# MoE1's second matmul by Strassen's seven products for eight of its twelve token chunks, and the other four chunks spread through MoE2

## The chip, the cores and the metric

One program on one core of a Trainium2 chip. The time is device microseconds of one execution; three executions of the kernel before gave 1471.46 to 1471.69 us, median 1471.59. A separate execution was profiled; its rows are shown below.

## The reference

Three stages in a row, all on float32 inputs and outputs (the MoE weights arrive as float64 words):

```python
scores = (1 / S) * z @ z.T                 # per batch; S = 3008, d_qk = 64
x = u * (maximum(scores, 0) ** 2 @ v)      # 2 x 3008 tokens, d_model = 256
h = maximum(x @ moe_w_in, 0)               # MoE1, d_ff = 2048
x = h * h @ moe_w_out
h = x @ moe2_w_in                          # MoE2, d_ff = 2048
y = (h - tanh(h)) @ moe2_w_out
```

## The kernel before

**Number format.** TensorE multiplies in a reduced float32 format (`F32R`). To keep accuracy every operand is split into a high part and a low part, and each product is three matmuls: high x high, low x high, high x low. The split costs a copy (ScalarE or VectorE) and a subtraction (VectorE) for each operand tile.

**Tiles.** The 6016 tokens are cut into 12 attention chunks (`chunks`, up to 512 tokens) and, for both MoE stages, into 12 even `groups`: four of 512 tokens and eight of 496. `d_ff` is cut into `NF` = 16 blocks of 128. One MoE step is a pair (chunk, block) and has two runs of six matmuls on TensorE:

- `front(i)` (L531): x times one block of w_in into one PSUM bank `s`, 2 halves of d_model x 3 terms;
- `back(i)` (L608): the block's activation `h` times w_out into the two accumulators `o` of the chunk, 2 halves of d_model x 3 terms.

Between them ScalarE and VectorE make `h` out of `s`. In MoE1: `bend` (L543, Relu out of PSUM, ScalarE), `power` (L546, Square, ScalarE), `high` (L589 on ScalarE or L591 on VectorE, the high part), `rest` (L594, the low part, VectorE). In MoE2 there are two activations and a square on ScalarE (L552, L543, L555), a difference, a mask, a product and a selection on VectorE (L560, L571, L579, L582), then `high` and `rest`; once MoE1 has no steps left the mask moves to ScalarE (L567).

**PSUM.** A core has eight banks of 512 float32 columns. In the MoE stages four serve `front` in rotation (pool `pf`), four serve as accumulators `o` (pool `po`).

**Order of the steps.** First all attention steps, then MoE1 and MoE2 steps: 41 MoE1 steps ahead, after which MoE2 and MoE1 steps alternate; 21 MoE2 steps remain alone at the end. MoE1's result of a chunk goes from PSUM straight into the split operand of MoE2 (`between`, L624 and L626).

**Who decides the order on each engine.** `plan` writes TensorE's order by hand (`order_p`): a front stands three steps ahead of its back (`LOOK`), four in the end. For the other engines it makes a `Job` for each operation with a due time, the pools that it takes and the work that it waits for, and `drive` lays them in order, engine by engine, by its own table of durations. The built program then holds a fixed order on each engine; nothing is decided at run time. An engine whose next instruction is not ready waits, and all behind it wait too.

**Weights.** Each weight block is loaded as float64 words, converted and split by a chain of three ScalarE and six VectorE instructions (`split_w`). The 16 blocks of MoE1 and ten of them by way of DRAM (`wd`) are prepared during attention and fetched back; MoE2's are prepared in the MoE stages.

Of the kernel before, what the change touches and what calls it, by code (L numbers as in the profile page):

```python
# [31 lines left out]
EARLY = 1  # L32
WARM = 13
# [9 lines left out]
def kernel(  # L43
# [40 lines left out]
    def width(kind, c):  # L84
        return chunks[c][2] if kind == "att" else groups[c][1]
# [63 lines left out]
    wd = dp.tile([KEEP0 + KEEP1, P, 2, 512], F32, name="wd")  # L149
# [8 lines left out]
    def load_v(b, j):  # L158

        if b == 0 and 3 <= j < 6:  # L160
            pool, tag = (wp, "w") if j == 5 else (rawp, "raw")
            raw = pool.tile([P, 2, D], F32, tag=tag, name="vraw")
        else:
            raw = ap_.tile([P, 2, D], F32, tag="a", name="vraw")
        if j < NV - 1:
# [27 lines left out]
    def split_z(b, t, raw):  # L193
# [4 lines left out]
        if b == t == 0:  # L198
# [30 lines left out]
    def split_w(m, f, keep, raw):  # L229
        if keep is None:  # L230
            w = wt["w", m, f] = wp.tile([P, 2, 512], F32R, tag="w", name="ww")
        else:
            if len(stage) < 2:
                stage.append(wp.tile([P, 2, 512], F32R, tag="w", name="wk"))
            w = stage[keep % 2]
        if w1_in.dtype == F32:
# [32 lines left out]
    def load_x(c):  # L269
        t0, n = groups[c]  # L270
        x = xp.tile([P, KD, NMAX], F32, tag="x", name="xr")
        SP.dma_start(out=x[:, :, :n], in_=xd[:, :, t0 : t0 + n])
        return x

    def split_x(c, x, u):
        t0, n = groups[c]
        if c >= EARLY:
            y = slice(max(done_u - t0, 0), n)
            yield "V", lambda: V.tensor_mul(x[:, :, y], x[:, :, y], u[:, :, y])
        xh, xl = new_xs(0, c)  # L280
# [6 lines left out]
    order = [(m, f) for m in range(2) for f in range(NF)]  # L287
    keeps = {STAY + k: k for k in range(KEEP0 + KEEP1)}
    split = STAY + KEEP0 + KEEP1

# [11 lines left out]
    end = at["m1", NCH - 1, NF - 1] + 1  # L302
    limit = (TC * math.tanh(TB * TH)) ** 2
# [94 lines left out]
    def opening(both):  # L398
# [4 lines left out]
        first("z", 1)  # L403
        A.activation(a[:, 0], a[:, 0], AF.Square)
        first("z", 1)
# [110 lines left out]

    def front(i):
        kind, c, k = steps[i]
        n = groups[c][1]
        if not single:  # L520
            s_pool.close()
            single["s"] = ctx.enter_context(
                tc.tile_pool(name="pf", bufs=4, space=bass.MemoryType.PSUM)
            )
        s = got[i] = single["s"].tile([P, NMAX], F32, tag="s", name="s")
# [90 lines left out]
    def between(c, d, e):  # L616

        n = groups[c][1]
        if d == 0 and e == "A":
            new_xs(1, c)  # L620
        xh, xl = xs[1, c]
        o = acc["m1", c][d][:, :n]
        if e == "A":
            A.activation(xh[:, d, :n], o, AF.Copy)  # L624
        else:
            V.tensor_sub(xl[:, d, :n], o, xh[:, d, :n])  # L626

    def out(c, d, e):

        n = groups[c][1]  # L630
        if d == 0:
            xt["y", c] = xp.tile([P, KD, NMAX], F32, tag="x", name="y")
        y, o = xt["y", c][:, d, :n], acc["m2", c][d][:, :n]
# [5 lines left out]
    def send(c):  # L639
# [4 lines left out]
            in_=xt["y", c][:, :, :n],  # L644
        )

    def send_last():
# [3 lines left out]
        y, o = xt["y", c], acc["m2", c]  # L651
        SP.dma_start(out=yT[:P, t0 : t0 + n], in_=y[:, 0, :n])
        A.activation(y[:, 1, :n], o[1][:, :n], AF.Copy)
        A.dma_start(out=yT[P:, t0 : t0 + n], in_=y[:, 1, :n])

    class Job:
# [26 lines left out]
        "f": [0.0] * 4,  # L683
# [38 lines left out]
    def best(e):  # L722
# [4 lines left out]
        if e == "P":  # L727
            return (max(free[e], ready(jobs[0])), jobs[0])
# [71 lines left out]
    def plan(first_steps):  # L800

        order_p, ahead = [], 2
        for n in range(at["m1", 0, 0]):
            until = min(n + (APART if n > 6 else 2), at["m1", 0, 0] - 1)
# [11 lines left out]
        ahead = at["m1", 0, 0]  # L816
        for n in range(ahead, len(steps)):
# [7 lines left out]
        for kind, i in order_p:  # L825
            when[kind, i] = t
            if kind[0] == "o":
# [89 lines left out]
        for k, (m, f) in enumerate(order):  # L917
# [8 lines left out]
            else:  # L926
                t0, t1 = when["f", at["m1", 0, 0]], when["f", at["m2", 0, 0]]
                need = t0 + 6.0 + (k - split + 1) * (t1 - t0 + 10.0) / (2 * NF - split)
                need, asks = min(need, when["f", at["m2", 0, f]] - 4.0), at["att", NCH - 1, 0] + 10
# [7 lines left out]
            fresh = kept is None or kept < 2  # L937
            owed[0] += fresh
# [6 lines left out]
            def begin(k, made=made, fresh=fresh):  # L945
                if k == 0:
                    owed[0] -= fresh
                made(k)
            jobs = chain(W, need, after, ["t", "t"] + ["w"] * fresh, give, begin)
            wjob[m, f] = jobs[-1]  # L950
            if kept is not None:
# [3 lines left out]
                last = (NCH - 1) * NV  # L955

                def bring(e, pools, m=m, f=f, kept=kept):
# [5 lines left out]
                    when["f", at["m1", 0, f]] - 12.0,  # L963
                    [(last + min(kept + 2, NV - 1), 0.0), (stages[-1], 0.0)],
                    ["w"],
                    S=2.6,
                )
        xjob, xhold = {}, {(m, c): hold("z") for m in range(2) for c in range(NCH)}
        for c in range(NCH):
            need = when["f", at["m1", c, 0]]  # L970
            x, u = [None], [None]
            xs_, us_ = hold("x"), hold(None)
            asks = at["m1", c - 1, 2] if c else (NCH - 1) * NV + 4

            def ask(e, pools, c=c, x=x):
                x[0] = load_x(c)

            def ask2(e, pools, c=c, u=u):
# [323 lines left out]
```

## Time and profile before

| | before |
|---|---|
| median of three executions | 1471.59 us |
| the profiled execution | 1471.73 us |
| its span in the trace | 1469.9 us |
| TensorE matmul busy | 1464.5 us |
| VectorE busy | 1232.2 us |
| ScalarE busy | 1070.1 us |
| granted TensorE clock | 1.00 of 2.4 GHz |

The profiled execution's time is 1.83 us above its span, which is the time that lies around the traced program. Busy time counts a stretch once, however many instructions of the engine overlap in it.

### The profile page before, as it was taken

What the parts mean: (1) busy time and instruction counts of PE and PEld (TensorE: products, weight loads), DVE (VectorE), ACT (ScalarE), POOL (GpSimd) and SP (SyncE); (2) the same over time, 40 slices, a digit from 0 to 9 for tenths busy, and PEclk for the clock granted to TensorE, in tenths of its full rate; (3) what the DMA queues carried; (4) which work ended last, traced back from release to release, by engine and by line L of the source; (5) the groups of instructions that cost most, each with busy time, mean ns of one, the idle gap of its engine ahead of it and who ended that gap; (6) DMA issues with size and microseconds to landing.
All of it is one profiled execution on the core that took longest, in us unless ns stands there. A gap on an engine that the chain in (4) does not pass through costs nothing.

```text
span 1469.9 us, 21919 instructions
## 1 busy us (share of the span) xinstructions
PE 1464.5 (100%) x8499; PEld 1230.9 (84%) x8499; DVE 1232.2 (84%) x1846; ACT 1070.1 (73%) x1698; POOL 0.3 (0%) x6
## 2 busy tenths in 40 slices
PE   9999999999999999999999999999999999999998
PEld 7888888888898888888888888888888888888887
DVE  7888999788986888877888888888888888888788
ACT  8987669987648987666666667676666766666688
POOL 0000000000000000000000000000000000000000
PEclk9999999999999999999999999999999999999999
DMA  8756648766663321010100100010101010000000
GB/s 256 249 193 219 207 154 262 266 216 212 218 244 95 119 91 38 1 42 1 43 1 1 42 1 15 1 42 1 42 1 43 1 42 1 14 1 15 1 14 15
DMA packets 74200, 125.67 MB, mean 85 GB/s; under 512 B 4720, under 2 KB 56688, under 8 KB 70256
## 3 DMA queue, kind: packets, MB, share of 16 engines
q1 hardware_dynamic: 73792, 123.76, 25.2%
q8 instruction: 66, 1.08, 0.3%
q10 hardware_dynamic: 304, 0.52, 0.1%
q14 instruction: 38, 0.31, 0.1%
HBM read 75.24 MB, written 49.02 MB: 85 GB/s over the span
## 4 chain that ended last, share of the span: by engine, by line
PE 96%; ACT 3%; DVE 1%; issue 0%
PE s L531 33%; PE o L608 33%; PE o L480 25%; PE s L431 4%; ACT h L589 1%; ACT least L567 1%; ACT a L543 1%; ACT f L552 0%; PE o L452 0%; ACT f L555 0%; PE s L1225 0%; DVE a L582 0%; PE s L416 0%; DVE a L560 0%; DVE g L579 0%
## 5 line engine op out<-in xcount | busy, mean ns | idle before, releaser
L608 PE MATMUL o<-h,ww 128*128 128x496 f32 (+1 forms) x2304 | 574.0, 385 | 0.4 <-DVE h L594 0.4
L531 PE MATMUL s<-xs,ww 128*128 128x496 f32 (+1 forms) x2304 | 573.9, 385 | 0.0
L608 PEld LDWEIGHTS o<-h,ww 128*128 128x128 f32 x2304 | 432.4, 188 | 80.3 <-DVE h L594 0.8
L531 PEld LDWEIGHTS s<-xs,ww 128*128 128x128 f32 x2304 | 432.3, 188 | 79.9 <-issue 0.3
L543 ACT ACTIVATE a<-s 128x496 f32<-128x496 f32 (+1 forms) x384 | 226.2, 589 | 155.7 <-PE s L531 154.1
L480 PE MATMUL o<-h,vw 64*128 64x512 f32 (+1 forms) x2240 | 339.3, 382 | 0.0
L594 DVE TENSOR_TENSOR h<-a,h 128x496 fp32r<-128x496 f32 (+1 forms) x384 | 248.4, 677 | 18.9 <-ACT h L589 14.7
L480 PEld LDWEIGHTS o<-h,vw 64*128 64x128 f32 x2240 | 209.9, 184 | 39.6
L560 DVE TENSOR_TENSOR a<-s,a 128x496 f32<-128x496 f32 (+1 forms) x192 | 130.3, 679 | 107.6 <-ACT a L543 106.7
L480 PE MATMUL o<-l,vw 64*128 64x512 f32 (+1 forms) x1120 | 214.1, 382 | 0.0
L552 ACT ACTIVATE f<-s 128x496 f32<-128x496 f32 (+1 forms) x192 | 114.1, 595 | 111.0 <-PE s L531 110.2
L589 ACT ACTIVATE h<-a 128x496 fp32r<-128x496 f32 (+1 forms) x219 | 136.9, 627 | 21.5 <-DVE a L582 8.2
L582 DVE COPY_PREDICATED a<-small,f 128x496 f32<-128x496 uint8 (+1 forms) x171 | 125.5, 734 | 5.1
L546 ACT ACTIVATE a<-a 128x496 f32<-128x496 f32 (+1 forms) x192 | 119.6, 623 | 5.6
L480 PEld LDWEIGHTS o<-l,vw 64*128 64x128 f32 x1120 | 105.0, 184 | 20.4 <-DVE l L371 0.8
L337 DVE STREAM_TRANSPOSE at<-m 128x1024 f32<-128x1024 f32 x60 | 121.8, 2030 | 0.0
L555 ACT ACTIVATE f<-f 128x496 f32<-128x496 f32 (+1 forms) x192 | 121.2, 631 | 0.0
L579 DVE TENSOR_TENSOR f<-s,f 128x496 f32<-128x496 f32 (+1 forms) x171 | 116.3, 680 | 5.1
L371 DVE TENSOR_TENSOR l<-a,h 128x1024 fp32r<-128x1024 f32 (+1 forms) x83 | 100.6, 1215 | 19.9 <-ACT h L362 19.5
L362 ACT ACTIVATE h<-at 128x1024 fp32r<-128x1024 f32 (+1 forms) x60 | 61.4, 1023 | 47.7 <-PE o L480 42.2
L591 DVE CAST h<-a 128x496 fp32r<-128x496 f32 (+1 forms) x165 | 69.1, 421 | 26.9 <-PE o L608 14.0
L393 ACT ACTIVATE a<-a 128x1024 f32<-128x1024 f32 (+1 forms) x83 | 87.3, 1054 | 1.3
(57 smaller groups left out, 824.3 us busy)
## 6 DMA issues: line engine op xcount, KB each, us to landing
ad<-a SPq DMA_DIRECT2D x60, 512.0 KB, 3.8
m<-ad SPq DMA_DIRECT2D x30, 1024.0 KB, 7.0
wraw<-in_moe_w_in_dram SPq DMA_DIRECT2D x32, 256.0 KB, 4.2
wraw<-in_moe_w_out_dram SPq DMA_DIRECT2D x32, 256.0 KB, 4.2
vraw<-in_v_dram SPq DMA_DIRECT2D x22, 256.0 KB, 4.8
wd<-wk SPq DMA_DIRECT2D x10, 512.0 KB, 4.3
ww<-wd SPq DMA_DIRECT2D x10, 512.0 KB, 9.5
xd<-e SPq DMA_DIRECT2D x9, 512.0 KB, 3.4
```

The costliest lines, as they stand in the source:

```text
L337: V.transpose(a.rearrange("p g (k j m) -> p m k g j", k=4, m=4), m.rearrange("p (m k) (t g i) -> t p m k g i", m=4, t=2, g=2)[p % 2],)
L480: T.matmul(o[r * KD + d][:, :n], lhsT=w[halves[r], hl, g * D + d * P : g * D + (d + 1) * P], rhs=mv[halves[r], g, :n], start=x == 0 and (r ...
L531: T.matmul(s[:, :n], lhsT=w[:, hl, kd * P : (kd + 1) * P], rhs=mv[:, kd, :n], start=j == 0, stop=j == len(seq) - 1,)
L543: A.activation(a, got[i][:, :n], func)
L546: A.activation(sq[i], sq[i], AF.Square)
L555: A.activation(fs[i], fs[i], AF.Square, scale=TC)
L560: V.tensor_sub(sq[i], got[i][:, :n], sq[i])
L579: V.tensor_mul(gs[i], got[i][:, :n], f)
L582: V.copy_predicated(sq[i], least[i], gs[i])
L589: A.activation(pair[i][:, 0], sq[i], AF.Copy)
L594: V.tensor_sub(pair[i][:, 1], sq[i], pair[i][:, 0])
L608: T.matmul(o[d][:, :n], lhsT=w[:, side, (KD + d) * P : (KD + d + 1) * P], rhs=mv, start=k == 0 and j % 3 == 0, stop=k == NF - 1 and j % 3 ...
```

## The change

Chunks 0 to 7 of MoE1 are taken in four pairs. For a pair, two blocks of d_ff and the two halves of d_model, the second matmul is a product of 2 x 2 blocks (two chunks by two blocks of d_ff, times two blocks of d_ff by two halves of d_model). Strassen's form (with Winograd's sums) makes it with seven block products in place of eight. A window ("w", r, j) is one such step: pair r of 4, block pair j of 8; there are 32.

A window has four fronts (L557, as before six matmuls each) and seven products (L632, three matmuls each). `rise` (L572 on ScalarE, L574 on VectorE) and `rise2` (L577) are the Relu and the Square; `less` (L581) makes the four differences of activations; `upper` (L588, or L590 on VectorE) and `lower` (L593) split each of the seven operands; `sums_w` makes the four sums of w_out blocks once for each j; `gather` (L647 to L667) combines the seven accumulators at the end of a pair, and `lay` stores the result to DRAM (`x2d`).

The seven accumulators take all four banks of `po` and three more (pool `pg`), so that one bank (`pf`) is left for the fronts of a window. After the phase, `many(i)` lets fronts rotate over `pg` and `pf` again.

The 64 MoE1 steps of chunks 8 to 11 are no longer alternating with MoE2 one to one: 16 stand ahead, the other 48 are spread over 167 of the 192 MoE2 steps (`LEAD`), and 25 MoE2 steps remain alone at the end. All of MoE1's results go to MoE2 through DRAM (`x2d`, `put_x`, `load_x`), and `between` is gone. Twelve of MoE2's weight blocks are converted in the new phase, four after it.

In the opening, scores of chunk 0 are recorded ahead of some loads, the second z tile's high part is a VectorE cast in place of a ScalarE copy, and a one-column memset holds back one load of v. In the ending, the last half of the output is copied by VectorE in two pieces that leave by two queues.

```diff
+PAIRS = 4
+DIRECT = 6
+LEAD = 16
+PRODUCTS = 1, 5, 7, 3, 6, 2, 4
+LATE = 3, 8, 14
...
     steps = [("att", c, x) for c in range(NCH) for x in range(NV)]
-    m1 = [("m1", c, k) for c in range(NCH) for k in range(NF)]
+    FFN = len(steps)
+    steps += [("w", r, j) for r in range(PAIRS) for j in range(NF // 2)]
+    m1 = [("m1", c, k) for c in range(2 * PAIRS, NCH) for k in range(NF)]
     m2 = [("m2", c, k) for c in range(NCH) for k in range(NF)]
-    lead = 2 * NF + LAG + 4
-    steps += m1[:lead]
-    given = lead
+    given = 0
     for i in range(len(m2)):
-        steps.append(m2[i])
-        ahead = lead - (NF + 4) * min(max(i - 2 * NF, 0), 8 * NF) // (8 * NF)
-        while given < min(len(m1), i + 1 + ahead):
+        while given < min(len(m1), LEAD + i * (len(m1) - LEAD) // (len(m2) - NF - LAG - 4)):
             steps.append(m1[given])
             given += 1
+        steps.append(m2[i])
...
+    def bank(many):
+        if not single:
+            s_pool.close()
+            for name, bufs in ((False, 1), (True, 3)):
+                single[name] = ctx.enter_context(
+                    tc.tile_pool(name="pg" if name else "pf", bufs=bufs, space=bass.MemoryType.PSUM)
+                )
+        return single[many].tile([P, NMAX], F32, tag="s", name="s")
...
+    def less(i, q, x, y):
+        V.tensor_sub(tiles[i, q], tiles[i, x], tiles[i, y])
...
+    def sums_w(j):
+        val = tp.tile([P, 512], F32, tag="t", name="val")
+        s = tp.tile([P, 512], F32, tag="t", name="sw")
...
+        yield "V", lambda: V.tensor_add(s1, a21, a22)
+        yield "V", lambda: V.tensor_sub(s3, a11, a21)
+        yield "V", lambda: V.tensor_sub(s2, s1, a11)
+        yield "V", lambda: V.tensor_sub(s4, a12, s2)
+        w = st[j] = wp.tile([P, 2, 512], F32R, tag="w", name="ws")
+        yield "A", lambda: A.activation(w[:, 0, :], s, AF.Copy)
+        yield "V", lambda: V.tensor_sub(w[:, 1, :], s, w[:, 0, :])
...
+    def product(i, p, part):
+        _, r, j = steps[i]
+        n = groups[2 * r][1]
+        if j == 0 and part == 0:
+            sb[r, p] = (
+                po.tile([P, NMAX], F32, tag="o", name="o") if p in (1, 5, 7, 3) else bank(True)
+            )
+        x = sb[r, p]
+        h = pair[i, p]
...
+        terms = ((0, h[:, 0]), (1, h[:, 0]), (0, h[:, 1]))
+        for y in (0, 1) if part == 0 else (2,):
+            hl, mv = terms[y]
+            T.matmul(
+                x[:, :n],
+                lhsT=w[:, hl, d * P : (d + 1) * P],
+                rhs=mv,
+                start=j == 0 and y == 0,
+                stop=j == NF // 2 - 1 and y == 2,
+            )
...
     def send_last():
...
-        A.activation(y[:, 1, :n], o[1][:, :n], AF.Copy)
-        A.dma_start(out=yT[P:, t0 : t0 + n], in_=y[:, 1, :n])
+        for way, cols in ((A, slice(0, n // 2)), (SP, slice(n // 2, n))):
+            V.tensor_copy(y[:, 1, cols], o[1][:, cols])
+            way.dma_start(out=yT[P:, t0 : t0 + n][:, cols], in_=y[:, 1, cols])
...
+        order_p += [(("f", q), FFN) for q in (0, 3, 1, 2)]
+        ahead = two
+        for n in range(FFN, two):
+            spots = {3: 0, 8: 1, 14: 2, 18: 3}
+            count = 0
+            for p in PRODUCTS:
+                for part in range(2):
+                    order_p.append((("p", p, part), n))
+                    count += 2 - part
+                    if count not in spots:
+                        continue
+                    if n + 1 < two:
+                        order_p.append((("f", spots[count]), n + 1))
```

What this makes of TensorE's order: before, in the 41 MoE1 steps ahead, a front of six and a back of six follow one another (the back alternates between the chunk's two accumulators, each row one matmul):

```order
L531 MATMUL s_6250<-xs_6075,ww_1479 128x512 x6
L608 MATMUL o_6209<-h_6219,ww_914 128x512
L608 MATMUL o_6210<-h_6219,ww_914 128x512
L608 MATMUL o_6209<-h_6219,ww_914 128x512
L608 MATMUL o_6210<-h_6219,ww_914 128x512
L608 MATMUL o_6209<-h_6219,ww_914 128x512
L608 MATMUL o_6210<-h_6219,ww_914 128x512
```

Now TensorE in one window of the third pair (`o_7425`, `o_7448`, `o_7455`, `o_7471`, `s_7479`, `s_7501`, `s_7518` are the accumulators of products 1, 5, 7, 3, 6, 2, 4; the other `s` are fronts, all in the one bank of `pf`):

```order
L632 MATMUL o_7425<-h_7565,ww_1244 128x496 x3
L557 MATMUL s_7631<-xs_7004,ww_5508 128x496 x6
L632 MATMUL o_7448<-h_7597,ws_5836 128x496 x3
L632 MATMUL o_7455<-h_7617,ws_5836 128x496 x2
L557 MATMUL s_7657<-xs_7170,ww_5508 128x496 x6
L632 MATMUL o_7455<-h_7617,ws_5836 128x496
L632 MATMUL o_7471<-h_7609,ws_5836 128x496 x3
L632 MATMUL s_7479<-h_7638,ws_5836 128x496 x2
L557 MATMUL s_7685<-xs_7170,ww_5536 128x496 x6
L632 MATMUL s_7479<-h_7638,ws_5836 128x496
L632 MATMUL s_7501<-h_7644,ww_1484 128x496 x3
L557 MATMUL s_7704<-xs_7004,ww_5536 128x496 x6
```

Between two fronts stand five, six and four matmuls of products (and, from the last front to the first of the next window, 3 + 3 = 6). The fronts belong to the next window, the products to this one. This pattern stands in 29 of the 32 windows; in three a product or a part of one has moved past a front.

VectorE at about the same place, where the operands of one window are made (`b` are activations, `wraw`, `mant`, `exp` and `wk` a weight block that is converted):

```order
L593 TENSOR_TENSOR h_7575<-b_7521,h_7575 128x496
L581 TENSOR_TENSOR b_7548<-b_7570,b_7548 128x496
L261 SCALAR_TENSOR_TENSOR exp_7394<-wraw_7052,exp_7394 128x512
L590 CAST h_7597<-b_7548 128x496
L264 TENSOR_TENSOR mant_7395<-mant_7395,exp_7394 128x512
L581 TENSOR_TENSOR b_7570<-b_7592,b_7570 128x496
L593 TENSOR_TENSOR h_7597<-b_7548,h_7597 128x496
L590 CAST h_7617<-b_7570 128x496
L581 TENSOR_TENSOR b_7548<-b_7592,b_7548 128x496
L593 TENSOR_TENSOR h_7617<-b_7570,h_7617 128x496
L593 TENSOR_TENSOR h_7609<-b_7592,h_7609 128x496
L593 TENSOR_TENSOR h_7638<-b_7548,h_7638 128x496
```

Before, VectorE had for the same MoE1 blocks only the low parts, one for each front, and sometimes a high part:

```order
L591 CAST h_6248<-a_6229 128x512
L594 TENSOR_TENSOR h_6248<-a_6229,h_6248 128x512
L594 TENSOR_TENSOR h_6260<-a_6243,h_6260 128x512
L594 TENSOR_TENSOR h_6287<-a_6269,h_6287 128x512
```

## Rows read from the trace of the kernel before

**Rows 1.** The page, part 1: span, and busy time, share, instructions of each engine.

```profile
span 1469.9 us, 21919 instructions
PE 1464.5 (100%) x8499; PEld 1230.9 (84%) x8499; DVE 1232.2 (84%) x1846; ACT 1070.1 (73%) x1698; POOL 0.3 (0%) x6
```

**Rows 2.** TensorE's waits after its first instruction: total us, times, longest.

```profile
PE o L608 <- DVE h L594: 0.4, 1, 0.4
PE s L431 <- ACT z L201: 0.4, 1, 0.4
```

**Rows 3.** Stages in time: busy us by engine, then PEclk, DMA share, GB/s.

```profile
441.00:1415.00 974.00, 974.00 (x4385) 821.96 (x4382) 799.50 (x1373) 681.12 (x1211) 0.00 (x0) 1.00 0.08 26
1415.00:1460.00 45.00, 45.00 (x206) 38.41 (x205) 44.24 (x74) 44.42 (x87) 0.00 (x0) 1.00 0.03 12
1460.00:1470.00 10.00, 6.01 (x26) 4.43 (x25) 4.79 (x9) 4.46 (x8) 0.00 (x0) 1.00 0.14 51
```

**Rows 4.** Timeline of TensorE and ScalarE, 512 then 496 tokens: start, us, instruction.

```profile
448.33 1.52 PE L531 MATMUL s<-xs,ww 128*128 128x512 f32 x6
449.69 1.52 PE L608 MATMUL o<-h,ww 128*128 128x512 f32 x6
449.89 0.60 ACT L543 ACTIVATE a<-s 128x512 f32<-128x512 f32 x1 [0.67 <-PE s L531]
...
1000.89 1.48 PE L608 MATMUL o<-h,ww 128*128 128x496 f32 x6
...
1002.21 1.48 PE L531 MATMUL s<-xs,ww 128*128 128x496 f32 x6
```

**Rows 5.** Groups of instructions by line: count, busy us, mean ns, idle before.

```profile
L608 PE MATMUL o<-h,ww 128*128 128x496 f32 (+1 forms) x2304 | 574.0, 385 | 0.4 <-DVE h L594 0.4
L594 DVE TENSOR_TENSOR h<-a,h 128x496 fp32r<-128x496 f32 (+1 forms) x384 | 248.4, 677 | 18.9 <-ACT h L589 14.7
L543 ACT ACTIVATE a<-s 128x496 f32<-128x496 f32 (+1 forms) x384 | 226.2, 589 | 155.7 <-PE s L531 154.1 <-DVE h L594 0.4
L589 ACT ACTIVATE h<-a 128x496 fp32r<-128x496 f32 (+1 forms) x219 | 136.9, 627 | 21.5 <-DVE a L582 8.2 <-PE o L608 4.2
L591 DVE CAST h<-a 128x496 fp32r<-128x496 f32 (+1 forms) x165 | 69.1, 421 | 26.9 <-PE o L608 14.0 <-ACT a L546 1.4 <-DVE a L582 0.5
L279 DVE TENSOR_TENSOR xr<-xr,u 128x992 f32<-128x992 f32 (+1 forms) x11 | 13.1, 1194 | 0.0
L281 ACT ACTIVATE xs<-xr 128x992 fp32r<-128x992 f32 (+1 forms) x12 | 12.5, 1038 | 0.0
```

**Rows 6.** Timeline of the end: TensorE's one wait for VectorE.

```profile
1458.93 3.68 PE L608 MATMUL o<-h,ww 128*128 128x496 f32 x16
...
1462.25 0.66 DVE L594 TENSOR_TENSOR h<-a,h 128x496 fp32r<-128x496 f32 x1
...
1462.96 2.98 PEld L608 LDWEIGHTS o<-h,ww 128*128 128x128 f32 x14 [0.76 <-DVE h L594]
1462.97 3.40 PE L608 MATMUL o<-h,ww 128*128 128x496 f32 x14 [0.36 <-DVE h L594]
```

**Rows 7.** VectorE's timeline, instructions back to back.

```profile
457.09 0.42 DVE L246 TENSOR_SCALAR exp<-wraw 128x512 uint32<-128x512 uint32 x1
457.43 1.29 DVE L594 TENSOR_TENSOR h<-a,h 128x512 fp32r<-128x512 f32 x2
458.63 0.69 DVE L249 SCALAR_TENSOR_TENSOR mant<-wraw,mant 128x512 f32<-128x512 uint32 x1
...
1436.33 0.67 DVE L579 TENSOR_TENSOR g<-s,f 128x496 f32<-128x496 f32 x1
1436.91 0.67 DVE L594 TENSOR_TENSOR h<-a,h 128x496 fp32r<-128x496 f32 x1
```

**Rows 8.** DMA issues: KB each, median us to landing.

```profile
xd<-e SPq DMA_DIRECT2D x9, 512.0 KB, 3.4
xr<-xd SPq DMA_DIRECT2D x8, 496.0 KB, 4.6
```

More of the change, by code (lines that the diff above doesn't have):

```diff
@@ L302 @@
     end = at["m1", NCH - 1, NF - 1] + 1
+    two = at["m1", 2 * PAIRS, 0]
+    st = {}
+    tiles = {}
+    sb = {}
+    ends = {}
     limit = (TC * math.tanh(TB * TH)) ** 2
@@ new lines, in enter @@
+    def enter(i, q):
+        c, f = corner(i, q)
+        n = groups[c][1]
+        s = got[i, q] = bank(i == FFN and q > 0)
+        w = wt["w", 0, f]
+        xh, xl = xs[0, c]
+        seq = [(hl, mv, kd) for hl, mv in ((0, xh), (1, xh), (0, xl)) for kd in range(KD)]
+        for y, (hl, mv, kd) in enumerate(seq):
+            T.matmul(
+                s[:, :n],
+                lhsT=w[:, hl, kd * P : (kd + 1) * P],
+                rhs=mv[:, kd, :n],
+                start=y == 0,
+                stop=y == len(seq) - 1,
+            )
@@ L517, in front, with lay @@
+    def lay(r, g):
+        t0, n = groups[2 * r + g]
+        SP.dma_start(out=x2d[:, :, t0 : t0 + n], in_=ends[r, "c", g][:, :, :n])
     def front(i):
@@ L519, in front @@
         n = groups[c][1]
[L520 to L525, printed above, removed]
+        s = got[i] = bank(many(i))
         m = 0 if kind == "m1" else 1
@@ L937, in plan @@
             fresh = kept is None or kept < 2
+            here = m == 1 and f < 2
             owed[0] += fresh
@@ new lines, in bring_x @@
+            xjob[m, c] = [(jobs[-3], 0.0), (jobs[-1], -0.8)]
+        for c in range(NCH):
+            if c < 2 * PAIRS:
+                r = c // 2
+                need = when[("f", c % 2), FFN + r * NF // 2]
+                asks = FFN + (r - 1) * NF // 2 + 1 + 2 * (c % 2) if r else (NCH - 1) * NV + 4
+            else:
+                need = when["f", at["m1", c, 0]]
+                asks = at["m1", c - 1, 2] if c > 2 * PAIRS else two - 5
+            t0, n = groups[c]
+            after = [
+                (("keep", k), 0.0)
+                for k, (b, q, m) in enumerate(chunks)
+                if t0 < b * S + q + m and b * S + q < t0 + n
+            ]
+            bring_x(0, c, need, asks, after)
@@ new lines, in plan, with made @@
+        shold, sjob = {}, {}
+        for j in range(NF // 2):
+            shold[j] = hold("w")
+            SW = [("V", 0.42)] * 2 + [("V", 0.25)] * 4 + [("A", 0.62), ("V", 0.69)]
+            todo = []
+            def made(k, j=j, todo=todo):
+                if k == 0:
+                    owed[0] -= 1
+                    todo.append(sums_w(j))
+                next(todo[0])[1]()
+            after = [(wjob[0, 2 * j], 0.0), (wjob[0, 2 * j + 1], 0.0)]
+            give = [(5, hold("t")), (7, hold("t"))]
+            sjob[j] = chain(
+                SW, when[("p", 5, 0), FFN + j] - 2.0, after, {0: ["t", "t"], 6: ["w"]}, give, made
+            )[-1]
@@ L1013, in forward, with begin @@
+    def begin(i, p):
+        if i == two - 2 and p == 1:
+            owed[0] += NF - 2
+        product(i, p, 0)
     def forward(kind, c, k, when, size, wjob, whold, xjob, xhold):
```

395 lines of the change are left out of this document (304 added, 91 removed).

## The prediction

> **What bounds the kernel now.** I read the page's busy line first. TensorE is busy for 1464.5 of 1469.9 us [rows 1]; the reader should see that no other engine could give time here unless TensorE does less. The view of waits confirms it: after its first instruction TensorE waits for anybody only twice, 0.4 us each [rows 2]. So the time is the number of matmuls times their spacing, plus whatever stalls a change brings. The windows come next, because an average hides stages: in the MoE stages from 441 to 1415 us VectorE is busy 799.5 of 974 us and ScalarE 681 [rows 3], so there is room; but in the last stretch of MoE2 steps alone, 1415 to 1460 us, VectorE has 44.2 and ScalarE 44.4 of 45 us, and TensorE still has all 45.00 [rows 3]. That row matters most here: engines that are 98% full do not by themselves make TensorE wait, as long as the fixed order suits. The spacing comes from the timeline: a block of six matmuls starts 1.36 us after the one before it at 512 tokens (0.2267 us each) and 1.32 us after it at 496 (0.22 each) [rows 4]. The group's mean of 385 ns [rows 5] is a matmul's latency, not its spacing, since they overlap.
>
> **The matmuls removed.** A window stands for four MoE1 steps. Their fronts stay (24 matmuls); their backs were 24 and are now 7 x 3 = 21. The built order shows it: 4608 matmuls of the MoE stages before, 4512 after, 3 x 32 = 96 fewer. Two pairs have 512 tokens, two 496: 48 x 0.2267 + 48 x 0.22 = **21.4 us less**. What is left of the phase is 1440 matmuls, 720 x 0.2267 + 720 x 0.22 = 321.6 us if TensorE never waits.
>
> **The one bank of the fronts.** Seven banks hold products, so the fronts share one, and a front can start only when the Relu has read the one before. The round trip from rows: ScalarE starts 0.20 us after the next block's first matmul (449.69 to 449.89) [rows 4]; the Relu out of PSUM takes 0.59 [rows 5]; a released matmul starts 0.06 after the release (1462.25 + 0.66 to 1462.97) [rows 6]. A stall costs more than the gap shown: the 14 matmuls after it are spaced (3.40 - 0.385) / 13 = 0.232, together 0.16 us over 0.22, because the weight load waited as well [rows 6]. In all 1.01 us. The order leaves 4, 5 or 6 product matmuls between fronts: 0.88, 1.10, 1.32 us at 496 tokens. Only the gap of four is too short, by 0.13 (by 0.11 at 512: 1.02 against 0.91). 16 x 0.13 + 16 x 0.11 = **3.8 us**. From below it is 0, if the weight load is not held (0.85 fits in 0.88). From above, if ScalarE is always half an instruction (0.3) late, the gaps of four and five lose 0.43 and 0.21, 0.64 x 32 = 20 us. I stay at 3.8, because ScalarE has room: 123 Relus x 0.589, 280 squares and high parts at 0.627 (the square is taken at the copy's duration, an estimate), 36 weight operations at the same price, seven splits of 1.04 and 14 other copies of about 0.6 come to 287 us, 89% of the phase, counted without any overlap [rows 5].
>
> The Trainium skill (Perfetto Trace Analysis, section Matmuls) speaks against this layout: independent groups should rotate through different banks, so that one's evacuation overlaps the next one's matmuls. Taken alone, with no credit for the products in between, it would expose 128 round trips of 1.01 us, an estimate of 129 us; by the rows it is 3.8, since those products write other banks meanwhile. No run so far shows which.
>
> **VectorE in the phase.** Back to back it starts an instruction every 0.60 us at 512 tokens, 0.58 at 496, and 0.34 for a cast or mask (457.09 to 457.43 to 458.63; 1436.33 to 1436.91) [rows 7]. Its rows in the phase by the built order, priced so: 224 low parts and 128 differences 208; 71 high parts 24; five Relus 3; twelve weight conversions (two at 0.34, four at 0.60 each) 37; seven gates at 1.19 - 0.09 and 14 low parts of x, 16; weight sums (24 small ones at no more than 0.34, and six low parts) 12; 21 gathers 12. Together 312 us for 572 rows: **97% of 321.6**. Before, the same MoE1 steps needed one low part for each front, about a third of that. What covers it: from the end of a window's third front to the first product that needs it (product 7 of the same window) 25 matmuls pass, 5.5 us, and the chain of Relu, square, difference, cast and low part takes 0.20 + 0.59 + 0.63 + 0.68 + 0.42 + 0.68 = 3.2. So VectorE may be some 2.3 us late, nearly four instructions, before TensorE notices; behind a late one stand all others in its queue, and so the next operands. The stretch of 98% without a stall [rows 3] says 0; a gather at a pair's end puts seven rows (4.1 us) into one window, which alone exceeds the 2.3. I take **2 us**, from 0 up to the rival below.
>
> **Edges.** At the phase's start the first chain is the old one with a difference in it; four fronts (5.4 us) cover 3.2 us after the first, so 0.5 us, from 0 to one front (1.4). At the end 25 MoE2 steps stand alone instead of 21, at the density of the 45 us above, and MoE1's last chunk now goes through DRAM. Between its last back and MoE2's first front of it stand 11 blocks, 14.5 us; the trip takes 0.20 + 2 x 0.59 + 3.4 + 4.6 + 1.04 + 0.68 = 11.1 [rows 5, 8], so it is hidden with 3.4 to spare; if both transfers took twice as long it would cost 4.6. For the denser ending I take **1 us** (0 to 4.6). MoE2 with fewer MoE1 steps has, priced as above, 613 us of VectorE to 681 of TensorE (90%), below the 98% that cost nothing: 0. In the opening the scores that waited 0.4 us for a ScalarE copy [rows 2] get it from VectorE: **-0.4** (or 0, if the held-back load of v is late). The ending's two half copies count 0 (at best -0.6, one copy's length).
>
> **Sum.** -21.4 + 3.8 + 2 + 0.5 + 1 - 0.4 = -14.5. Against the profiled execution's own 1471.73 us that is 1457.2; that execution lies 0.14 above the median of the runs, which changes nothing here.
>
> **Rivals.**
>
> *All hidden.* The fronts' gap of four suffices and VectorE's lag stays under 2.3 us: 1471.7 - 21.4 - 0.4 = 1450 us, up to 1452. For it speaks the 45 us stretch; against it, the 0.13 us that the gap lacks.
>
> *VectorE becomes the bound (the other side).* An instruction that needs a fresh result of ScalarE cannot start 0.09 us before the one ahead ends, and waits besides; VectorE's order here switches between the two engines' results in nearly every row. If each row costs its full duration [rows 5], the phase needs 352 x 0.68 + 71 x 0.42 + 5 x 0.69 + 12 x 3.6 + 18 + 14 + 14 = 362 us. It was 321.6 + 21.4 = 343 for the same work before, so the result is 1471.7 + 19 = 1491. It decides from the point where the mean row passes 343 / 572 = 0.60 us instead of the 0.547 above: 0.05 us of idle or lost overlap for each row. Against it: in the dense stretch VectorE's idle is 0.76 us in 74 rows, 0.01 each [rows 3], and the order still puts two thirds of the high parts on ScalarE.
>
> *Most of it eaten.* Both the fronts' bank and VectorE at half their upper bounds: +10 and +10, 1471.7 - 21.4 + 20 + 1 = about 1471, no change.
>
> *The clock falls.* TensorE's granted clock is 1.00 (2.4 GHz) in every row, also in the last 10 us where TensorE is busy for 6.0 [rows 3]. If frequent short stalls lowered it to 1.2 GHz for a tenth of the phase, 144 matmuls would take 0.22 us more each: 32 us, net 1489. The Trainium skill (TensorE: Matmul & The Clock Gate, section on psum-queue depth-cycling) reports just such a kernel, in which cycling through PSUM banks made short idles and the clock swung between its levels. The stalls expected here are a few per cent of the phase at most, so I give it little.
>
> That the change does not do what it says is excluded by the count of matmuls in the built order.
>
> **Chances.** Forecast (1452 to 1464.5) 0.58; all hidden 0.16; more eaten but still faster (1464.5 to 1468.6) 0.07; within 0.2% (2.9 us, about what a measurement of this kernel can tell from no change) 0.06; VectorE the bound 0.10; the clock 0.03. So faster 0.81, same 0.06, slower 0.13. The range reaches down to the hidden case, 1450, and up to 1467, which leaves out some 0.2, most of it above.
>
> **What would show it.** Right: about 4512 matmuls of lines 557, 632, 683 and 760, in a phase of some 328 us from about 441 us on; TensorE's waits in it some 6 us, most on fronts (L557) released by the Relu L572, the rest on products (L632) released by L593; VectorE near 95% busy in the phase; nothing waiting for `xr`. Wrong: waits of L632 on VectorE of 20 us and more with VectorE at 100% (the second rival); PEclk under 1.00 (the clock); stalls in MoE2 that wait for `xs` (the trip through DRAM); or no waits on L557 at all (all hidden).

## The result, and the profile after

The changed kernel takes **1457.78 us** (median of four executions, 1457.50 to 1458.19) against 1471.64 for the kernel before beside it: ratio 0.9908, 95% interval 0.9893 to 0.9922, so 13.9 us less. The prediction was 1457.2. Below, "window" is one of the 32 steps of the new phase, and "bare" is what its matmuls take at the spacing of [rows 4]: 45 x 0.2267 = 10.20 us at 512 tokens, 45 x 0.22 = 9.90 at 496.

The page's span and busy line, which answer to [rows 1]:

```profile
span 1455.8 us, 22202 instructions
PE 1449.8 (100%) x8403; PEld 1215.0 (83%) x8403; DVE 1351.0 (93%) x2117; ACT 1146.6 (79%) x1845; POOL 0.3 (0%) x6
```

TensorE loses 96 matmuls and 14.7 us; VectorE's busy time grows by 118.8 us. In TensorE's waits after its first instruction (total us, times, longest), which answer to [rows 2], the only one that comes from the phase is 0.2 us, although its windows are late by more, as will be seen:

```profile
PE o L760 <- DVE h L746: 0.7, 1, 0.7
PE s L557 <- ACT b L572: 0.2, 1, 0.2
```

The same view for the weight loads between 440 and 772 us shows what the matmul rows hide. There are 32 waits for the Relu, about one for each window:

```profile
PEld s L557 <- ACT b L572: 7.2, 32, 0.7
PEld s L632 <- DVE h L593: 0.4, 1, 0.4
PEld s L557 <- issue: 0.3, 1, 0.3
PEld s L557 <- DVE b L574: 0.3, 1, 0.3
```

Busy time in the phase (440 to 780) and in 100 us of MoE2 (columns as in [rows 3]):

```profile
440.00:780.00 340.00, 339.63 (x1500) 277.42 (x1499) 328.58 (x599) 273.50 (x478) 0.00 (x0) 1.00 0.25 82
940.00:1040.00 100.00, 100.00 (x447) 83.48 (x445) 94.89 (x167) 78.04 (x144) 0.00 (x0) 1.00 0.05 18
```

VectorE is busy for 97% of the phase, the clock stays at 1.00. TensorE's timeline (start, us, instruction), a window at 512 tokens and a front at 496:

```profile
546.35 1.52 PE L557 MATMUL s<-xs,ww 128*128 128x512 f32 x6
547.71 0.39 PE L632 MATMUL s<-h,ws 128*128 128x512 f32 x1
547.94 0.84 PE L632 MATMUL s<-h,ww 128*128 128x512 f32 x3
548.62 1.59 PE L557 MATMUL s<-xs,ww 128*128 128x512 f32 x6
550.05 0.86 PE L632 MATMUL s<-h,ww 128*128 128x512 f32 x3
...
693.74 1.50 PE L557 MATMUL s<-xs,ww 128*128 128x496 f32 x6
695.08 1.28 PE L632 MATMUL o<-h,ws 128*128 128x496 f32 x5
```

Between the fronts at 546.35 and 548.62 stand four product matmuls, the short gap. The front behind it takes 1.43 us to the next block instead of the 1.36 of the other front: 0.07 lost, with 0.02 more in the blocks around it. And at 496 tokens a front takes 695.08 - 693.74 = 1.34 us, 0.2233 per matmul, where [rows 4] have 1.32 and 0.22. The phase's end:

```profile
770.92 0.39 PE L632 MATMUL s<-h,ws 128*128 128x496 f32 x1
771.14 2.07 PE L632 MATMUL s<-h,ww 128*128 128x496 f32 x6
773.30 1.60 PE L683 MATMUL s<-xs,ww 128*128 128x496 f32 x6
```

The last six products take 2.16 us to the next block, 0.84 over bare; the front behind them waits for a bank that a gather (L655) frees.

**Where the 6.6 us of the phase went.** From the first front (441.13) to the first front after the phase (773.30) are 332.17 us for 1458 matmuls, 18 of them of plain MoE1; bare 720 x 0.2267 + 738 x 0.22 = 325.6. From window to window (start of the first product to the next one's): at 512 tokens 10.97 once, 10.69 and 10.38 once each, the other twelve 10.28 to 10.31; at 496 mostly 10.10. That is: fronts' bank 15 x 0.09 at 512 and 0.7 at 496, together **2.0**; wider spacing at 496, 720 x 0.0033 = **2.4**; three irregular windows (0.77 + 0.49 + 0.18 - 3 x 0.09) **1.2**; start and end (0.15 + 0.84) **1.0**.

Two of the three irregular windows come from the built order. Where a product stands behind the front that it usually precedes, a gap is shorter than four: two matmuls in the first window and three in the ninth. By the round trip of 1.00 us (below, e2) they lack 0.55 and 0.32 us, some 0.8 beyond the 0.09 that every window loses. So this part of the 1.2 belongs to the one bank too.

### The profile page after: what moved, and what is told of

Read it like the earlier page. It is cut to its first block, busy times and chain, and to the rows that moved or that the text cites. A ratio compares the mean times of both kernels' runs of the same rounds, so it can differ in the third digit from the quotient of the medians.

```text
span 1455.8 us, 22202 instructions
## 1 busy us (share of the span) xinstructions
PE 1449.8 (100%) x8403; PEld 1215.0 (83%) x8403; DVE 1351.0 (93%) x2117; ACT 1146.6 (79%) x1845; POOL 0.3 (0%) x6
## 4 chain that ended last, share of the span: by engine, by line
PE 99%; DVE 0%; ACT 0%; issue 0%; DVEq 0%
PE o L493 26%; PE s L683 23%; PE o L760 23%; PE s L557 12%; PE o L632 6%; PE s L632 4%; PE s L444 4%; PE o L465 0%; PE s L1575 0%; PE s L429 0%; DVE l L386 0%; DVE e L510 0%; DVE a L712 0%; DVE h L593 0%; DVE a L734 0%; ACT h L588 0%
## 5 line engine op out<-in xcount | busy, mean ns | idle before, releaser
L760 PE MATMUL o<-h,ww 128*128 128x496 f32 (+1 forms) x1392 | 346.1, 384 | 0.7 <-DVE h L746 0.7
L683 PE MATMUL s<-xs,ww 128*128 128x496 f32 (+1 forms) x1392 | 346.4, 384 | 0.1
L760 PEld LDWEIGHTS o<-h,ww 128*128 128x128 f32 x1392 | 261.2, 188 | 48.5 <-DVE h L746 1.1
L683 PEld LDWEIGHTS s<-xs,ww 128*128 128x128 f32 x1392 | 261.2, 188 | 47.9 <-DVE c L655 0.4
L557 PE MATMUL s<-xs,ww 128*128 128x512 f32 (+1 forms) x768 | 195.3, 390 | 0.2 <-ACT b L572 0.2
L746 DVE TENSOR_TENSOR h<-a,h 128x496 fp32r<-128x496 f32 (+1 forms) x256 | 171.1, 674 | 13.7 <-ACT h L741 11.8
L557 PEld LDWEIGHTS s<-xs,ww 128*128 128x128 f32 x768 | 141.6, 188 | 34.2 <-ACT b L572 7.2
L741 ACT ACTIVATE h<-a 128x496 fp32r<-128x496 f32 (+1 forms) x207 | 128.9, 624 | 45.0 <-DVE a L734 39.6
L695 ACT ACTIVATE a<-s 128x496 f32<-128x496 f32 (+1 forms) x256 | 149.6, 584 | 14.8 <-PE s L683 14.1
L593 DVE TENSOR_TENSOR h<-b,h 128x512 fp32r<-128x512 f32 (+1 forms) x224 | 145.5, 678 | 4.8 <-ACT h L588 3.6
L572 ACT ACTIVATE b<-s 128x496 f32<-128x496 f32 (+1 forms) x123 | 72.9, 592 | 56.1 <-PE s L557 54.3
```

The source lines that it names most:

```text
L557: T.matmul(s[:, :n], lhsT=w[:, hl, kd * P : (kd + 1) * P], rhs=mv[:, kd, :n], start=y == 0, stop=y == len(seq) - 1,)
L593: V.tensor_sub(pair[i, p][:, 1], tiles[i, q], pair[i, p][:, 0])
L683: T.matmul(s[:, :n], lhsT=w[:, hl, kd * P : (kd + 1) * P], rhs=mv[:, kd, :n], start=j == 0, stop=j == len(seq) - 1,)
L695: A.activation(a, got[i][:, :n], func)
L741: A.activation(pair[i][:, 0], sq[i], AF.Copy)
L746: V.tensor_sub(pair[i][:, 1], sq[i], pair[i][:, 0])
```

## The experiments

Each was timed in three rounds beside the kernel before, whose medians were 1471.2 to 1471.7.

**e1: a second bank for the fronts.** Product 4 adds into product 2's accumulator, which frees a bank.

```diff
-            for name, bufs in ((False, 1), (True, 3)):
+            for name, bufs in ((False, 2), (True, 2)):
...
-                po.tile([P, NMAX], F32, tag="o", name="o") if p in (1, 5, 7, 3) else bank(True)
+                sb[r, 2] if p == 4 else po.tile([P, NMAX], F32, tag="o", name="o") if p in (1, 5, 7, 3) else bank(True)
```

> Product 4 adds into product 2's accumulator, so six banks hold products and the fronts of a window have two (that part of the result is not the reference's; the count of matmuls is the same). Theory, the one bank costs: in the changed kernel a window of 45 matmuls takes 10.29 us at 512 tokens instead of 10.20 and 10.10 at 496, and the fronts' weight loads wait 32 times for the Relu, 7.2 us in all. With two banks these waits go, the window of 512 takes 10.20, and the time falls by 2.3 us (1.5 to 3.5), to about 1455.5. Rival, late operands of VectorE set the loss: unchanged within 0.5 us, 1457.8.

1452.16 us (1451.79 to 1454.08), ratio 0.9871 (0.9857 to 0.9886): 5.6 less than the change. (The traced execution is the one of 1454.08; it spends 5.9 us behind its last matmul, the change's 3.7.) The windows are bare, 10.20 and 9.90 (the first 10.25), the weight loads' waits on L572 are gone, and so are, in the phase, the irregular windows and the wider spacing at 496. So the bank is the cause of more than the 2.0 that stand under its own name. The plan also takes four high parts and two Relus off VectorE, some 2.6 us; e3, which takes off far more, gains only 1.5, so that is not the 5.6. The same gap of four matmuls now costs nothing (columns as above):

```profile
544.45 1.52 PE L557 MATMUL s<-xs,ww 128*128 128x512 f32 x6
545.81 0.39 PE L632 MATMUL s<-h,ws 128*128 128x512 f32 x1
546.03 0.84 PE L632 MATMUL s<-h,ww 128*128 128x512 f32 x3
546.72 1.52 PE L557 MATMUL s<-xs,ww 128*128 128x512 f32 x6
548.08 0.84 PE L632 MATMUL s<-h,ww 128*128 128x512 f32 x3
```

**e2: a gap of three.** One matmul less in the short gap of each window.

```diff
-            spots = {3: 0, 8: 1, 14: 2, 18: 3}
+            spots = {3: 0, 8: 1, 14: 2, 17: 3}
```

> The fourth front of a window stands one matmul earlier: the gap of four matmuls becomes three, the next one seven instead of six; nothing else is changed. Theory, the one bank costs: the round trip is the same, its cover is 0.22 to 0.23 us shorter, so each window takes 0.22 us more: 32 x 0.22 = 7 us, about 1465. Rival, VectorE sets the loss: no change, 1457 to 1459.

1464.57 (1464.16 to 1464.82), ratio 0.9953 (0.9938 to 0.9968): 6.8 more than the change. Windows take 10.52 and 10.32; 31 x 0.22 = 6.8. The matmul taken out of the gap is lost whole, so the round trip is longer than three matmuls: at 512 tokens 3 x 0.2267 + 0.32 = 1.00 us, and 4 x 0.2267 + 0.09 = 1.00 by the change itself; at 496, in the wider spacing, 3 x 0.2233 + 0.27 = 0.94, and 4 x 0.2233 + 0.05 = 0.94.

**e3: less VectorE.** Products 2 and 6 use the high part in place of a low part, which leaves out 64 VectorE instructions.

```diff
-        terms = ((0, h[:, 0]), (1, h[:, 0]), (0, h[:, 1]))
+        terms = ((0, h[:, 0]), (1, h[:, 0]), (0, h[:, 0 if p in (2, 6) else 1]))
...
+            if p in (2, 6):
+                lo[p] = hi[p]
+                return hs
```

> Products 2 and 6 multiply the high part twice; their low parts are left out (64 of VectorE's 572 rows in the phase, some 38 us; that part of the result is not the reference's). Theory, the one bank costs and VectorE's lag is covered: 1457 within 1 us, windows as before (10.29 and 10.10). Rival, VectorE at 97% sets the loss: the phase loses most of its 6.6 us over the bare matmuls, about 1452.

1456.29 (1455.57 to 1456.35), ratio 0.9895 (0.9879 to 0.9912): 1.5 less. The ordinary windows stay at 10.29 and 10.10; what goes is the 10.69, part of the 10.97, and most of the stall at the phase's end. So a lighter VectorE is worth 1.5 us to the change. The edit does not reach VectorE alone: the plan answers with 83 high parts on VectorE instead of 72 and so 11 fewer on ScalarE, and in the ninth window, the 10.69, it lays the usual gaps of five, six and four matmuls.

**e4: parts of one matmul, gaps of 5, 5, 5 and 6.** A product is placed in three parts, so that no gap has fewer than five.

```diff
-LATE = 3, 8, 14
+LATE = 3, 8, 13
...
-        for y in (0, 1) if part == 0 else (2,):
+        for y in (part,):
...
-            spots = {3: 0, 8: 1, 14: 2, 18: 3}
+            spots = {3: 0, 8: 1, 13: 2, 18: 3}
...
-                for part in range(2):
+                for part in range(3):
```

> Each product is laid down as three parts of one matmul instead of parts of two and one, so that the third front can stand after 13 matmuls instead of 14 and the gaps are 5, 5, 5, 6 instead of 5, 6, 4, 6; the result is unchanged. Theory, the one bank costs: gaps of five (1.13 and 1.10 us) cover the round trip of some 1.0, the waits go as with two banks, about 1455.5. Rival, VectorE sets the loss: unchanged within 0.5 us, 1457.8.

1459.23 (1459.10 to 1459.34), ratio 0.9917 (0.9902 to 0.9932): a miss, 1.45 more than the change instead of 2.3 less. Windows of 512 tokens are bare or far off (10.20 to 10.90). By its built order e4 also gives VectorE ten high parts more than the change, 82 for 72, and two Relus less. ScalarE's timeline at one of the late ones, with a row of TensorE (start, us, idle before and what ended it):

```profile
478.72 1.06 ACT L290 ACTIVATE xs<-xr 128x1024 fp32r<-128x1024 f32 x1 [0.30 <-DVE xr L288]
479.93 0.63 ACT L588 ACTIVATE h<-b 128x512 fp32r<-128x512 f32 x1
480.34 1.29 PE L632 MATMUL o<-h,ws 128*128 128x512 f32 x5
480.46 0.62 ACT L577 ACTIVATE b<-b 128x512 f32<-128x512 f32 x1
480.98 0.58 ACT L572 ACTIVATE b<-s 128x512 f32<-128x512 f32 x1
```

The block behind this front began at 480.34, so by [rows 4] its Relu could start at 480.54. It started at 480.98, behind a split (L290) that had waited for VectorE's gate (L288), a high part and a square. A late VectorE thus holds the fronts' bank through ScalarE's fixed order, and the wait then carries ScalarE's name. That is a theory from one place; e5 and e6 test it.

**e5: more VectorE.** The low parts of products 2 and 6 are written twice.

```diff
-        V.tensor_sub(pair[i, p][:, 1], tiles[i, q], pair[i, p][:, 0])
+        for _ in range(2 if p in (2, 6) else 1):
+            V.tensor_sub(pair[i, p][:, 1], tiles[i, q], pair[i, p][:, 0])
```

> Every low part of products 2 and 6 in the phase is written twice: 64 VectorE rows more, the same result, and TensorE's and ScalarE's orders and VectorE's other rows are unchanged. By back-to-back pricing the phase then asks 312 + 64 x 0.60 = 350 us of VectorE in 332. Theory (VectorE has room until its demand passes the phase's own length, then every row costs its 0.60): the room of 20 us is used up first, so 350 - 332 = 18 us, and 15 to 27 us slower than the change. Rival A (VectorE was the bound already and each row costs at its full 0.68): 44 us slower. Rival B (VectorE still has slack to spare, the bank of the fronts alone sets the pace): within 3 us of the change.

1493.51 (1493.34 to 1493.78), ratio 1.0149 (1.0132 to 1.0166): a miss, 35.7 more than the change, 0.56 per instruction, above the 15 to 27 of the theory and below rival A's 44. VectorE had no room of 20 us, but at 0.60 us per instruction 64 x 0.60 - 35.7 = some 3. The phase's busy time and the weight loads' waits from 440 to 810 us (the kernel's lines are one higher than the change's from L594 on):

```profile
440.00:780.00 340.00, 318.53 (x1360) 250.06 (x1357) 334.64 (x602) 249.28 (x433) 0.00 (x0) 0.99 0.20 67
```

```profile
PEld s L557 <- ACT b L572: 35.0, 52, 2.2
PEld s L557 <- DVE b L574: 6.3, 4, 1.9
PEld s L633 <- DVE h L594: 2.2, 4, 0.8
```

Only VectorE got more work, VectorE is at 98%, ScalarE is less busy than before (249 for 274), and yet the waits name ScalarE's Relu. Waits on the low parts themselves (L633 on L594) are small.

**e6: thirds with less VectorE.** The edits of e3 and e4 together.

```diff
-        for y in (0, 1) if part == 0 else (2,):
+        for y in (part,):
...
+            if p in (2, 6):
+                lo[p] = hi[p]
+                return hs
```

> The thirds of e4 (five or six product matmuls between any two fronts) and the lighter VectorE of e3 (products 2 and 6 use their high part in place of a low part, so that part of the result isn't the reference's). Theory (thirds lost because a late VectorE holds up ScalarE's fixed queue and with it the Relu that frees the fronts' bank): with VectorE lighter the windows of 512 tokens all take 10.20 us, those of 496 between 9.90 and 10.05, and the time is 1451 to 1454. Rival A (the order of thirds is itself worse, whatever VectorE does): 1457 to 1459, as the sum of the two runs, 1457.8 + 1.45 - 1.5. Rival B (the weight load is held whatever the gap): 1456.

1453.08 (1452.90 to 1453.37), ratio 0.9875 (0.9860 to 0.9890): as the theory had it, and not the sum of the two single effects (1457.7). But the plan gives VectorE 101 high parts here for e4's 82, so ScalarE has 19 fewer, 12 us at 0.63, and e6 alone doesn't tell a late VectorE from a late ScalarE; e10 does. Windows of 512 tokens take 10.20 to 10.25 apart from the first, 10.75; at 496 nine take 9.90, and then six 10.05.

**e7 and e8: five pairs, and two.**

```diff
-PAIRS = 4
+PAIRS = 5
```

> Five pairs in place of four: 24 matmuls of the backs fewer, 5.3 us. Theory (the loss is per window, so it grows with the pairs): eight windows more at 0.09 to 0.20 us each cost 1 to 1.6, so 1453.5, between 1452.5 and 1455. Rival (MoE2, with 17 steps of MoE1 left over to cover... namely 16, ends with more of its dense steps alone): 1456 to 1460.

> Two pairs in place of four, both of 512 tokens: 48 matmuls more than the change, 48 x 0.22 = 10.6 us. Theory (loss per window plus a fixed cost of the phase's two edges of about 2 us): half the windows' loss comes back, so 1457.8 + 10.6 - 2 = 1466, between 1464.5 and 1468. Rival (the loss is in the phase's edges and in MoE2, not in the windows): 1468 to 1470.

Five pairs: 1465.61 (1465.45 to 1465.81), ratio 0.9960 (0.9945 to 0.9975), a miss: 7.8 more than the change with 24 matmuls less. The phase runs as with four (10.29, 10.10). The loss is in MoE2, which now has only two chunks of MoE1 to mix in; busy time there, and the largest sum of the weight loads' waits from 860 to 1460 us:

```profile
940.00:1040.00 100.00, 98.96 (x432) 80.14 (x431) 98.45 (x173) 81.38 (x148) 0.00 (x0) 1.00 0.07 22
```

```profile
PEld o L760 <- DVE h L746: 11.3, 27, 1.0
```

With four pairs the same view of MoE2 (774 to 1445) has no wait at all, at 94.89 of 100. From the phase's end on, e7's matmuls take 13.6 us more than bare, the change's 1.4: 7.5 of the 13.6 are late matmuls, and 5.8 are the wider spacing, which e7 has from 1139 us to the end and for 30 us before. Two pairs: 1489.40 (1487.78 to 1489.89), ratio 1.0120 (1.0105 to 1.0135), a miss that says nothing of the dose: the built order of the last pair has from none to 12 matmuls between its fronts, and TensorE is busy for 17 of 20 us there (560 to 620). It is another order, not half a change.

**e9 and e10: thirds, with high parts moved to ScalarE.** e9 takes VectorE's price out of the planner's job for a high part, e10 raises it.

```diff
                 A=A63,
-                V=V42,
+                V=V69,
```

> The thirds of e4, and every high part of a product's operand is copied by ScalarE (224 of 224, where e4 gave VectorE 101 of them); the result is the same. VectorE's demand falls by some 101 x 0.34 = 34 us, ScalarE's rises by 101 x 0.63 = 64 to about 94% of the phase. Theory (a late VectorE was what held up the Relus of e4): windows of 10.20 us at 512 tokens, 1452 to 1455. Rival (ScalarE, now the fuller one, is late itself and the fronts wait for its Relu): 1458 to 1466, with waits of the fronts on the Relu as the largest.

> As e9, but the planner still may give a high part to VectorE, at a price of 0.69 in place of 0.42: 59 of 224 go there, and one half of the Relus' four less; the result is the same. Theory: VectorE falls by 42 x 0.34 + 1.8 = 16 us, most of what e6 took away (38), so most of the windows take 10.20 us and the time is 1453 to 1456. Rival (only the full 38 us of e6 free the Relus): as e4, 1458 to 1460.

(By the built orders e4 gives VectorE 82 high parts; 101 is e6's number. So e9 takes away 28 us, and e10 8 and two Relus.) e9: 1457.31 (1456.86 to 1459.31), ratio 0.9907 (0.9893 to 0.9922), between the two expectations: its first window takes 12.04, where its built order has gaps of three, three and four, and others are off by 0.03 to 0.25, with ScalarE at 303 of 340 us. **e10: 1455.00** (1454.03 to 1455.80), ratio 0.9889 (0.9872 to 0.9905), as its theory had it: of its fifteen periods at 512 eleven are 10.20 and two 10.22 and 10.23. ScalarE has 23 high parts and two Relus more here than in e4 and the fronts are still freed in time, which speaks for VectorE as what made e4 late. e10 computes the same as the change, and its times and the change's do not overlap: 2.8 us faster, the best version that does.

**e11 and e12: the widths in another order.** e11 is e6 with the four 512-token chunks last; e12 is e10 with them as chunks 0, 1, 4 and 5.

```diff
-    even = [16 * (B * S // 16 // NCH + (c < B * S // 16 % NCH)) for c in range(NCH)]
+    even = [16 * (B * S // 16 // NCH + (c >= NCH - B * S // 16 % NCH)) for c in range(NCH)]
```

> As e6 (thirds, products 2 and 6 without their low part, so that part of the result isn't the reference's), but the four chunks of 512 tokens are the last four, so that all eight of the phase have 496. The same matmuls in number and columns. Theory A (the wider spacing of 0.2233 in place of 0.22 at 496 tokens sets in at an irregular moment and then stays until a block of 512 comes): windows of 9.90 us up to some pair's boundary and 10.05 from there to the phase's end, 1453 to 1457. Theory B (it belongs to a place late in the phase): only the windows of the last pair take 10.05, and the time is that of e6, 1453. Theory C (it has nothing to do with the width): it shows nowhere, 1451 to 1452.

> As e10 (same result as the change), with the widths of the eight chunks of the phase ordered 512, 512, 496, 496, 512, 512, 496, 496, so that the pairs alternate. The same matmuls in number and columns. Theory (a window of 512 tokens ends the wider spacing, and a boundary from 512 to 496 does not begin it, as in e10 between its second and third pair): both pairs of 496 run at 9.90 us per window, 8 x 0.15 = 1.2 us less than e10, so 1453.8, between 1453 and 1455. Rival (it begins at any late boundary): 496 windows of the fourth pair at 10.05, 1455.

e11: 1457.17 (1456.87 to 1457.86), ratio 0.9904 (0.9890 to 0.9919). All windows but the first take 10.05, from the start, which none of its three theories had, with 0.9 us of weight-load waits in the whole phase; the wider spacing ends when blocks of 512 tokens come. A front and five products of e11, then of e10:

```profile
600.28 1.28 PE L632 MATMUL o<-h,ws 128*128 128x496 f32 x5
601.40 1.50 PE L557 MATMUL s<-xs,ww 128*128 128x496 f32 x6
602.74 1.05 PE L632 MATMUL o<-h,ws 128*128 128x496 f32 x4
```

```profile
662.45 1.26 PE L632 MATMUL o<-h,ws 128*128 128x496 f32 x5
663.55 1.48 PE L557 MATMUL s<-xs,ww 128*128 128x496 f32 x6
664.87 1.04 PE L632 MATMUL o<-h,ws 128*128 128x496 f32 x4
```

The same instructions in the same order, 1.34 against 1.32 for the front. e12: 1455.28 (1454.80 to 1456.06), ratio 0.9892 (0.9875 to 0.9908), no gain over e10. Both pairs of 496 begin at a spacing of 0.22 and change to 0.2233 (10.05 per window), one in its first window (533 us) and one in its fourth (725 us), not at a boundary. Theory and rival both fail on where it begins; the last section says what the traces show there.

## Why the prediction was right, and where its steps were not

**Matmuls, -21.4.** Right: 4512 left (768 + 672 + 1536 + 1536), and the spans agree: -21.4 + 6.6 in the phase - 0.3 in the opening + 1.0 behind the phase = -14.1, and 1455.8 - 1469.9 = -14.1. Predicted were 6.3 in the phase, -0.4 and 1, so the sums agree in each stage; inside the phase the terms do not, and that they add up so well is in part luck.

**The fronts' one bank, 3.8.** The mechanism and the round trip were right (1.02 us at 512 predicted, 1.00 by the change and by e2), and so was the place, the gap of four. At 496 tokens it was 0.94 for 1.01, so the gap of four lost 0.05 there and not 0.13. The size was too low: the gaps of four cost 2.0, but the bank costs 5.6 when it is taken away (e1). The traces show most of the rest: 0.8 for the two gaps of two and three, which the prediction did not count, and the 2.4 of the wider spacing, which begins behind a front's late weight load (last section). The Trainium skill (Perfetto Trace Analysis, section Matmuls) asks that independent groups rotate through different banks. e1 agrees on the sign, with 5.6 us; the 129 us, every round trip exposed, do not show.

**VectorE in the phase, 2.** The number stands (e3: 1.5); the step behind it failed. "Together 312 us" was too low, and room in busy time is not room for work: from the first front to the phase's end VectorE is busy for 321.0 of 332.2 us, so 11 us are idle, yet e5 shows room for some 3, where 332 - 312 would leave 20. VectorE stands just short of being the bound: 64 low parts fewer give 1.5 us, 64 more cost 35.7. This term came out because the change stops just short of it, which the prediction did not know. And the sign by which the second rival was to be known, waits of products on VectorE of 20 us, was wrong: in e5 the waits are the fronts', on ScalarE's Relu.

**MoE2, 0.** Right for the change, but not for its reason. The "98% that cost nothing" of [rows 3] is no rule: with VectorE at 98% over 400 us of MoE2, e7 loses 13.6 us against bare.

**The wider spacing, not foreseen.** 2.4 us in the phase and some 0.6 in the plain MoE1 steps behind it, until about 812 us. The prediction had its sign in hand: in [rows 6] it read 0.232 us per matmul behind the one stall and took that as a cost of the stall, once. The sum was near because this stood in for what the gaps of four had too much (3.8 for 2.0).

**Edges.** Start 0.5: 0.15 and most of the first window's 0.77. The end of the phase (0.84) was not in the sum. Opening -0.4: the phase begins at 441.13, where MoE1 began at 441.39 before, -0.3. That gain is not shown: the engines' orders in the opening are the same in all 13 traces of changed kernels, and their phases begin anywhere from 440.96 (e7) to 442.05 (e12), at a median of 441.58. Ending 1: TensorE's last wait is 0.7 for 0.4, so 0.3; the rest of the 1.0 behind the phase is mostly the wider spacing.

**Rivals.** All hidden (1450) fails on the gaps of four, 0.09 us per window at 512 tokens; e6 comes near it with VectorE relieved. VectorE as the bound fails for the change and holds 64 instructions further on. "Most of it eaten" fails: the phase loses 6.6 us, not 20. The clock is 1.00 in the change as long as matmuls run; of all traces only e5 shows a fall before the last matmul (below). The Trainium skill (TensorE: Matmul & The Clock Gate, section on psum-queue depth-cycling) tells of a kernel whose clock swung with such short idles. The change doesn't agree: 32 waits in the phase, and the clock stays.

**The signs.** The phase is 332 us long for 328, VectorE is at 97% for 95%, nothing waits for `xr`, and the fronts wait for the Relu as foretold. But they do so in the weight loads, 7.2 us, where TensorE's matmul rows, which the prediction named, show 0.2.

## What to carry to other kernels

In a pipeline with fixed orders on every engine, read which engine is near 100% in the stage before believing the name in a wait: an engine that is late shows under the name of the one whose queue it holds up. Two tight resources (a single bank, a full VectorE) are not additive; relieve both or measure both together, as e3, e4 and e6 show. Where a planner lays the orders, count the instructions of each engine again after every edit: here it moved high parts between engines in most of the runs. Count what sits between a release and the next use in matmuls, and look at weight loads as well as matmuls: waits of 7.2 us there were 0.2 us in the matmul rows.

## What the hardware showed that was not expected

**Two spacings at 496 tokens.** The same matmuls run at 0.22 or at 0.2233 us, at granted clock 1.00, for hundreds of us, in e11 without a wait between. In e11, e12 and the change the wider one ends when 512-token blocks come. Where it begins, a weight load had come late: its idle time before, 0.03 us in the narrow spacing, is longer at each beginning in the phases of all traces. Weight loads (start, us, idle before) in the change, in e10, in e11's first window and at the end of e1's phase, each at the beginning of a wide stretch:

```profile
610.25 1.19 PEld L557 LDWEIGHTS s<-xs,ww 128*128 128x128 f32 x6 [0.19 <-ACT b L572]
693.41 1.19 PEld L557 LDWEIGHTS s<-xs,ww 128*128 128x128 f32 x6 [0.41 <-ACT b L572]
441.55 2.53 PEld L557 LDWEIGHTS s<-xs,ww 128*128 128x128 f32 x12 [0.31 <-issue]
767.13 0.19 PEld L632 LDWEIGHTS s<-h,ww 128*128 128x128 f32 x1 [0.41 <-DVE h L593]
```

At 496 tokens e1 has no such wait before 766 us and no wide stretch; from 767 us to its first block of 512 tokens it has one. e12's two begin behind idle times of 0.18 and 0.09 us. Not every late load begins one, and some end it: the change is back at 0.22 from 630.5 to 640.5 us, between two waits of 0.20. In e9 one ends at 658 us without a wait or a block of 512. At 512 tokens a stall is followed by some six matmuls of up to 0.236 us (449.6 and 535.9 in the change), and then 0.2267 is back. Why 496 columns do not recover stays open.

**The clock after one stall.** In e5 TensorE idled 1.78 us before a front, and the granted clock then fell to 0.50 of 2.4 GHz (1.2 GHz). TensorE's timeline, then three windows (columns as above):

```profile
641.48 2.19 PE L557 MATMUL s<-xs,ww 128*128 128x496 f32 x6 [1.78 <-ACT b L572]
643.47 1.44 PE L633 MATMUL s<-h,ww 128*128 128x496 f32 x3
644.71 1.28 PE L633 MATMUL o<-h,ww 128*128 128x496 f32 x3
645.83 1.51 PE L557 MATMUL s<-xs,ww 128*128 128x496 f32 x6
```

```profile
640.00:642.00 2.00, 0.52 (x2) 0.49 (x3) 2.00 (x5) 1.63 (x3) 0.00 (x0) 1.00 0.55 204
643.00:644.00 1.00, 1.00 (x4) 0.77 (x3) 1.00 (x3) 0.29 (x1) 0.00 (x0) 0.50 0.67 250
646.00:648.00 2.00, 2.00 (x10) 1.68 (x10) 1.97 (x4) 1.03 (x3) 0.00 (x0) 1.00 0.79 301
```

Twelve matmuls took 4.35 us instead of 2.68. An idle stretch of 1.51 us earlier in the same phase (584.7) was followed by none. The fall shows no price in the time: the four executions have a mean clock of 0.999, 1.000, 1.000 and 0.999 at 1493.78, 1493.57, 1493.34 and 1493.44 us.
